# Scale s and offset b moved from the hidden values to the outputs, in a kernel of chunked attention and a squared-ReLU layer

## The chip, the cores and the metric

The kernel runs on one core of a Trainium2 chip. A core has a matrix engine (TensorE, in the profile PE, with its weight loads as PEld), a vector engine (VectorE, DVE), an engine for pointwise functions (ScalarE, ACT), a general engine (GpSimd, POOL) and an engine that here only issues DMAs (SyncE, SP). Each engine works through its own instructions in the order in which they were written and waits on semaphores for the others. The metric is the device time of one execution in microseconds (us); lower is better. The profile speaks of the span, which runs from the first to the last instruction of one profiled execution.

## The reference, cut to what matters

```
# attention: 4 batches, 8 heads, 768 positions of 64; chunks of 32 queries,
# each sees 16 positions to the left, its own 32, 8 to the right, and 8 memory slots
scores = scale * q_c @ k_full.T ;  a = softmax(scores) ;  attn = a @ v_full
x = attn as (3072 tokens, 512)
# the layer
h = x @ w_in                    # 512 -> 2048
r = maximum(h, 0)
g = s * (r * r) + b             # s and b are single numbers
out = g @ w_out                 # 2048 -> 512
```

Since s and b are single numbers, g @ w_out equals s * ((r * r) @ w_out) + b * (column sums of w_out). Nothing in the reference changes; this identity is what the change rests on.

## The kernel before, in words

**Tiling.** The 3072 tokens are eight chunks of 384 (`TOK`), and the 2048 hidden values are sixteen blocks of 128 (`NF`). A step is a pair (chunk, block). `STEPS` runs chunk 0 with blocks 0 to 7, then chunk 1 with all sixteen, then chunk 0 with blocks 8 to 15, then chunks 2 to 7 with all sixteen: 128 steps. In a step, `hidden(u)` makes the 128 x 384 hidden block on PE (L510, 12 matmuls of 384 columns), and ACT takes it through relu (L517), square (L518), s and b (L519, called affine) and a rounding to the short float type into gH (L520). DVE then makes the rest gL, which is the block minus gH (L521). `result(u)` multiplies gH and gL by the block's 128 rows of w_out and adds into three accumulator banks, one for each 128 tokens (L532, 9 matmuls of 512 columns). Every matrix stands as a high and a low part of the short float type, so that three products give nearly full precision: low times high, high times low, high times high.

**Order on PE.** `result` comes one `hidden` late: in steady work the order is hidden(k), result(k-1), hidden(k+1), result(k). So between the end of hidden(k) and the start of result(k) PE has a result and a hidden of other steps to do, while ACT and DVE make gH(k) and gL(k).

**Weights.** Both matrices arrive as 64-bit floats. For each of the 32 blocks of 128 rows (sixteen of each matrix, `weight()`), a DMA brings the words into one of four `words` buffers (the first ten use other space, `early`), and five instructions join the two halves into a 32-bit float and split it: ACT scales (L487), DVE shifts, joins and sets the sign (L488, L490, L492), ACT rounds into the high part (L496), and DVE subtracts to get the low part (L497). These blocks are made while chunks 0 and 1 are already computed.

**Attention.** For each chunk and pair of heads: scores on PE (L383), mask and row maximum on DVE (L440, two instructions for each of eight tiles), exp with row sums on ACT (L444), a small add on POOL (L447), a reciprocal on DVE (L449), the division on POOL (L450, called norm, 96 x 512), a transposition (on PE for chunks 0 and 1, on DVE for the later ones, L470), the value product on PE (L415), and the split into xH and xL (L419 on ACT, L420 on DVE).

**What sets the order.** The program hands all operations to a planner (`Plan`), each with its engine, a hold time from a table (`HOLD`), a due time, the values it reads and writes, and sometimes a flag `lock`. `lay()` walks through time and on each free engine starts the ready operation with the smallest due time; the instructions are then written in the order of their planned starts. With `lock`, an operation of DVE and one of POOL are not started while the other's locked one is running in the plan. The flag is on POOL's L447 and L450 and on DVE's four weight operations. It only orders: no semaphore keeps the two apart on the chip. Tiles come from rings with a fixed number of buffers and are given out in the order in which the values were created. The eight banks of PSUM are one ring `ps` whose function `room` limits each kind: accumulators three, hidden blocks (h) two, scores (s) and attention values (v) together three.

**End of a chunk.** When a chunk's last step is done, DVE copies the three accumulators out (L548) and SP writes them. Chunk 0 is broken in two: after its block 7 ACT stores the partial sums (L543), and after block 15 DVE adds them to the second half (L550).

Of the kernel before, what the change touches and what calls it, by code (L numbers as in the profile page):

```python
# [47 lines left out]
LEAD = 3.5  # L48
BANKS = 8
ORDER = sorted((f + half, half, f) for f in range(NF) for half in range(2))  # L50
LATE_W = [x[1:] for x in ORDER[-NEARLY:]]

# [8 lines left out]
            low=475, affine_v=475, rec=120, max=212, flip=316, xlow=470, wlow=345, wjoin=610, wsign=612, out=600,  # L61
            small=240, norm=1010, wrest=1290, issue=440)
LATE = dict(PE=230, ACT=180, DVE=180, POOL=150, SP=0)
# [182 lines left out]
def body(ctx: ExitStack, tc: tile.TileContext, qkv, w1, w2, out):  # L246
# [7 lines left out]
    def ring(name, n, shape, dtype):  # L254
        return Ring([const.tile(shape, dtype, name=f"{name}{i}") for i in range(n)])
# [27 lines left out]
    gs = Ring([(const.tile([P, TOK], F32R, name=f"gH{i}"), const.tile([P, TOK], F32R, name=f"gL{i}")) for i in range(3)])  # L283
    outs = ring("partial", 3, [P, DM], F32)

    spare = [BANKS - 1]

# [20 lines left out]

    c_id, c_aT, c_mask, c_s, c_b = (fixed() for _ in range(5))
    op("ACT", "copy", -100, lambda: nc.scalar.activation(s_sb, ones[:, :1], AF.Exp), (), (c_s[0],))  # L310
# [188 lines left out]


    g_vals, h_vals, a_vals, partial = {}, {}, {}, {}

    def hidden(u):
        ch, f = STEPS[u]
        h = Val(ps, "h")
        x, w = x_vals[ch], c_w[0, f]

        def products(c):
            for n, (wi, xi) in enumerate(((0, NC_T + c), (1, c), (0, c))):
                nc.tensor.matmul(h.tile[:, :TOK], weight_tile(0, f)[:, wi, c * P:(c + 1) * P], x.tile[xi], start=(c == 0 and n == 0),  # L510
                                 stop=(c == NC_T - 1 and n == 2))

        for c in range(NC_T):
            op("PE", "hidden", u, lambda c=c: products(c), (x["H", c], x["L", c], w["H"], w["L"]), (h[0],))
        g = g_vals[u] = Val(gs)
        hp = lambda: h.tile[:, :TOK]
        op("ACT", "relu", u, lambda: nc.scalar.activation(hp(), hp(), AF.Relu), (), (h[0],))  # L517
        op("ACT", "square", u, lambda: nc.scalar.activation(hp(), hp(), AF.Square), (), (h[0],))  # L518
        op("ACT", "affine", u, lambda: nc.scalar.activation(hp(), hp(), AF.Identity, scale=s_sb, bias=b_sb), (c_s[0], c_b[0]), (h[0],))  # L519
        op("ACT", "high", u, lambda: nc.scalar.activation(g.tile[0], hp(), AF.Copy), (h[0],), (g["H"],))  # L520
        op("DVE", "low", u, lambda: nc.vector.tensor_tensor(g.tile[1], hp(), g.tile[0].bitcast(F32), ALU.subtract),  # L521
           (h[0], g["H"]), (g["L"],))

    def result(u):
# [9 lines left out]
        for t in range(NT):  # L534
# [6 lines left out]
            if f < NF - 1:  # L541
                o = partial[t] = Val(outs)
                op("ACT", "store", u, lambda acc=acc, o=o: nc.scalar.activation(o.tile, acc.tile, AF.Copy), (acc[0],), (o[0],))  # L543
                continue
            o = partial[t] if not ch else Val(wvs if ch == 1 else outs)
            ot = lambda o=o: o.tile
            if ch:
                op("DVE", "out", u, lambda acc=acc, ot=ot: nc.vector.tensor_copy(ot(), acc.tile), (acc[0],), (o[0],))  # L548
            else:
                op("DVE", "out", u, lambda acc=acc, ot=ot: nc.vector.tensor_tensor(ot(), acc.tile, ot(), ALU.add), (acc[0],), (o[0],))  # L550
            row = ch * TOK + t * P
# [6 lines left out]
    for i, (due, half, f) in enumerate(ORDER):  # L558
        weight(i, half, f, due - 1.5)
    for u, (ch, f) in enumerate(STEPS):  # L560
        if ch not in made:
# [52 lines left out]
```

## Time and profile before

| what | value |
|---|---|
| three timed runs | 641.42, 642.25, 642.20 us; median 642.2 |
| span of the profiled execution | 639.8 us |
| what lies around a span | 1.6 us to the fastest run, 2.4 us to the median; the profiled execution's own time is not listed |
| ACT busy | 422.4 us (66%), of which the affine (L519) 82.6 us |
| DVE busy | 354.8 us (55%) |
| POOL busy | 86.9 us (14%) |
| granted TensorE clock | 1.000 |

A row of the groups view names line, engine, operation, output<-inputs, the shape and the count, and then busy us, mean ns of one, idle time of the engine just before them and what ended it. A row of the timeline gives the start in us, the duration in us, engine, line, operation, and in square brackets the idle time before it with its releaser. Matmuls are pipelined: the starts of successive matmuls say more than their durations, and the same holds for DVE, where an instruction starts about 0.1 us before the one ahead of it is over.

### The profile page before, as it was taken

The numbers are of one execution on the slowest core, as the hardware profiler recorded it, in microseconds if no ns is written. First come the engines' busy times: TensorE is split into PE (matmuls) and PEld (weight loads), VectorE is DVE, ScalarE is ACT, GpSimd is POOL, SyncE is SP. The second block draws the span as 40 slices with busy tenths as digits, with TensorE's granted clock in tenths as the row PEclk, the third lists the DMA queues.
The fourth block names the chain that finished last, engine by engine and source line by source line (L and its number), as shares of the span: only waits on it lengthen the run. The fifth ranks groups of instructions, "written<-read, shape, count | busy, mean of one in ns | idle before, by whom it ended". The sixth has DMA issues, their size and how long they took to land.

```text
span 639.8 us, 10842 instructions
## 1 busy us (share of the span) xinstructions
PE 625.7 (98%) x3822; PEld 544.2 (85%) x3826; DVE 354.8 (55%) x1283; ACT 422.4 (66%) x1137; POOL 86.9 (14%) x140
## 2 busy tenths in 40 slices
PE   9998988999999999999999999999999999999997
PEld 5686877888888898888888988889888888989995
DVE  5999999726667355563447554473555725421112
ACT  6999898756766566666566666664666665645543
POOL 4522100101211011110011111110111100100000
PEclk9999999999999999999999999999999999999999
DMA  8933664012112011121103011120111200010001
GB/s 336 404 112 114 212 207 152 2 46 83 58 46 96 5 41 47 47 95 47 45 2 105 37 46 46 46 96 1 45 47 47 96 17 1 1 50 1 1 0 50
DMA packets 17334, 46.83 MB, mean 73 GB/s; under 512 B 1920, under 2 KB 1920, under 8 KB 17280
## 3 DMA queue, kind: packets, MB, share of 16 engines
q1 hardware_dynamic: 17280, 46.15, 20.8%
q8 instruction: 30, 0.49, 0.3%
q14 instruction: 24, 0.20, 0.1%
HBM read 39.85 MB, written 6.29 MB: 72 GB/s over the span
## 4 chain that ended last, share of the span: by engine, by line
PE 80%; DVE 10%; ACT 6%; DMA 4%; issue 1%; SPq 0%; POOL 0%; DVEq 0%
PE ps L532 37%; PE ps L510 36%; PE ps L383 4%; PE ps L415 3%; DVE wv L490 2%; DVE w L497 2%; DVE wv L492 2%; DMA early<-w 2%; ACT t L444 1%; DMA v<-qkv 1%; DVE gL L521 1%; DVE words L488 1%; ACT wv L487 1%; DMA early<-qkv 1%; ACT ps L519 1%; ACT w L496 1%
## 5 line engine op out<-in xcount | busy, mean ns | idle before, releaser
L510 PE MATMUL ps<-xH,w 128*128 128x384 f32 x1024 | 261.8, 337 | 1.3 <-DVE w L497 1.3
L532 PE MATMUL ps<-w,gH 128*128 128x512 f32 x768 | 240.0, 393 | 0.6 <-DVE w L497 0.5
L510 PEld LDWEIGHTS ps<-xH,w 128*128 128x128 f32 x1024 | 186.0, 188 | 7.6 <-DVE w L497 2.4
L521 DVE TENSOR_TENSOR gL<-ps,gH 128x384 fp32r<-128x384 f32 x128 | 70.6, 552 | 208.8 <-ACT gH L520 207.6
L517 ACT ACTIVATE ps<-ps 128x384 f32<-128x384 f32 x128 | 60.9, 475 | 173.1 <-PE ps L510 173.1
L510 PE MATMUL ps<-xL,w 128*128 128x384 f32 x512 | 174.4, 341 | 0.0
L532 PEld LDWEIGHTS ps<-w,gH 128*128 128x128 f32 x768 | 144.0, 188 | 29.4 <-DVE w L497 1.3
L532 PE MATMUL ps<-w,gL 128*128 128x512 f32 x384 | 154.9, 403 | 6.6 <-DVE gL L521 6.6
L470 DVE STREAM_TRANSPOSE aT<-t 32x128 f32<-32x128 f32 x384 | 116.2, 303 | 51.1 <-POOL t L450 46.4
L444 ACT ACTIVATE t<-t,nmax 96x128 f32<-96x128 f32 x256 | 99.3, 390 | 17.2 <-DVE nmax L440 16.9
L510 PEld LDWEIGHTS ps<-xL,w 128*128 128x128 f32 x512 | 96.1, 188 | 6.6 <-ACT w L496 0.4
L532 PEld LDWEIGHTS ps<-w,gL 128*128 128x128 f32 x384 | 72.0, 188 | 24.5 <-DVE gL L521 9.6
L519 ACT ACTIVATE ps<-ps,b_sb,s_sb 128x384 f32<-128x384 f32 x128 | 82.6, 645 | 4.2
L450 POOL TENSOR_TENSOR t<-t,rden 96x512 f32<-96x512 f32 x64 | 68.5, 1070 | 85.8 <-DVE rden L449 85.8
L447 POOL TENSOR_SCALAR rden<-den 96x4 f32<-96x4 f32 x64 | 16.0, 251 | 375.5 <-ACT t L444 372.8
L520 ACT ACTIVATE gH<-ps 128x384 fp32r<-128x384 f32 x128 | 62.9, 491 | 3.9
L518 ACT ACTIVATE ps<-ps 128x384 f32<-128x384 f32 x128 | 60.8, 475 | 4.0
L440 DVE CUSTOM_DVE_ANT_0 t<-ps,mask 96x128 f32<-96x128 f32 x256 | 56.8, 281 | 4.2 <-PE ps L383 3.8
L444 ACT ACTIVATION_READ_ACCUMULATOR t<-t,nmax 96x1 f32 x256 | 48.1, 188 | 0.0
L383 PE MATMUL ps<-raw 64*96 64x128 f32 x448 | 31.8, 279 | 0.0
L383 PEld LDWEIGHTS ps<-raw 64*96 64x96 f32 x448 | 25.3, 159 | 4.1 <-issue 0.8
L415 PEld LDWEIGHTS ps<-aT,v 128*64 128x64 f32 x448 | 19.6, 136 | 7.9 <-issue 6.6
(45 smaller groups left out, 289.3 us busy)
## 6 DMA issues: line engine op xcount, KB each, us to landing
raw<-qkv SPq DMA_DIRECT2D x28, 448.0 KB, 3.3
words<-w SPq DMA_DIRECT2D x22, 512.0 KB, 3.9
v<-qkv SPq DMA_DIRECT2D x28, 256.0 KB, 3.6
out<-partial SPq DMA_DIRECT2D x21, 256.0 KB, 2.1
early<-w SPq DMA_DIRECT2D x10, 512.0 KB, 9.9
early<-qkv SPq DMA_DIRECT2D x3, 448.0 KB, 5.8
early<-qkv SPq DMA_DIRECT2D x4, 256.0 KB, 6.4
out<-wv SPq DMA_DIRECT2D x3, 256.0 KB, 3.8
```

The source lines that it names most:

```text
L383: nc.tensor.matmul(scv(n)[:, j, :], raw.tile[rows, j * QB:(j + 1) * QB], raw.tile[rows, TOK + j * P:TOK + (j + 1) * P], start=True, stop=True)
L440: op("DVE", "max", a + 0.1, lambda j=j: nc.vector.tensor_tensor_reduce(t.tile[:, j, :], scv()[:, j, :], mask[:, kind(j)], -SCALE, 3.0e38, ...
L444: op("ACT", "exp", a + 0.2, lambda j=j: nc.scalar.activation(t.tile[:, j, :], t.tile[:, j, :], AF.Exp, bias=nmax()[:, j:j + 1], scale=-1.0 ...
L450: op("POOL", "norm", a + 0.25, lambda: nc.gpsimd.tensor_tensor(t.tile, t.tile, rden().unsqueeze(2).to_broadcast([QB, GB, P]), ALU.mult), [ ...
L470: nc.vector.transpose(aT.tile[gg, :, cs], t.tile[cs, :, gg])
L510: nc.tensor.matmul(h.tile[:, :TOK], weight_tile(0, f)[:, wi, c * P:(c + 1) * P], x.tile[xi], start=(c == 0 and n == 0), stop=(c == NC_T - ...
L517: op("ACT", "relu", u, lambda: nc.scalar.activation(hp(), hp(), AF.Relu), (), (h[0],))
L518: op("ACT", "square", u, lambda: nc.scalar.activation(hp(), hp(), AF.Square), (), (h[0],))
L519: op("ACT", "affine", u, lambda: nc.scalar.activation(hp(), hp(), AF.Identity, scale=s_sb, bias=b_sb), (c_s[0], c_b[0]), (h[0],))
L520: op("ACT", "high", u, lambda: nc.scalar.activation(g.tile[0], hp(), AF.Copy), (h[0],), (g["H"],))
L521: op("DVE", "low", u, lambda: nc.vector.tensor_tensor(g.tile[1], hp(), g.tile[0].bitcast(F32), ALU.subtract), (h[0], g["H"]), (g["L"],))
L532: nc.tensor.matmul(acc.tile, g.tile[gi][:, t * P:(t + 1) * P], weight_tile(1, f)[:, wi, :], start=(first and n == 0), stop=(last and n == 2))
```

## The change

- L519, the affine on ACT, is gone from every step. The block that goes to `result` is now just the square.
- s is multiplied in where an accumulator leaves PSUM: in the copy of chunk 0's partial sums on ACT, and in the output instruction on DVE, which becomes a scalar_tensor_tensor (accumulator times s plus a tile).
- The tile `bc` holds b times the column sums of w_out, the same in all 128 partitions. It is made once, by the new function `sums()`: fifteen additions on POOL, of 128 x 1024 each (high and low part side by side), add the sixteen blocks of w_out into a tile `total` from the ring `words`; two matmuls with a matrix of ones ("columns") add over the partitions into one PSUM bank; and one activation on ACT multiplies by b into `bc`.
- That bank has a kind of its own, `"sum"`, so that it stands in no queue with the value banks; in `room` it falls under the last line, the one for hidden blocks.
- The outputs of chunks 1 to 7 add `bc` in the DVE instruction. Chunk 0's second half adds its partial sums there, so `bc` is added by POOL in a further instruction of 128 x 512 for each of three tiles, and SP writes the tile after that.
- The planner's table gets `sum=2150` and `columns=1706`, and all these operations have the due time `DUE_SUM = 24.0`, step 24 being the first after chunk 1. The fifteen additions and the three later ones carry `lock`.

```
+DUE_SUM = 24.0
...
+    def sums():
+        total, all_ = Val(words), Val(ps, "sum")
+        flat = lambda f: weight_tile(1, f).bitcast(F32).rearrange("p a n -> p (a n)")
+        part = lambda f: (c_w[1, f]["H"], c_w[1, f]["L"])
+        op("POOL", "sum", DUE_SUM, lambda: nc.gpsimd.tensor_tensor(total.tile, flat(0), flat(1), ALU.add), part(0) + part(1), (total[0],), lock=True)
+        for f in range(2, NF):
+            op("POOL", "sum", DUE_SUM, lambda f=f: nc.gpsimd.tensor_tensor(total.tile, total.tile, flat(f), ALU.add), part(f), (total[0],), lock=True)
+        def products():
+            for a in range(2):
+                nc.tensor.matmul(all_.tile, ones_f, total.tile[:, a * DM:(a + 1) * DM], start=a == 0, stop=a == 1)
+        op("PE", "columns", DUE_SUM, products, (total[0],), (all_[0],))
+        op("ACT", "store", DUE_SUM, lambda: nc.scalar.activation(bc, all_.tile, AF.Identity, scale=b_sb), (all_[0], c_b[0]), (c_bc[0],))
...
-        op("ACT", "affine", u, lambda: nc.scalar.activation(hp(), hp(), AF.Identity, scale=s_sb, bias=b_sb), (c_s[0], c_b[0]), (h[0],))
...
-                op("ACT", "store", u, lambda acc=acc, o=o: nc.scalar.activation(o.tile, acc.tile, AF.Copy), (acc[0],), (o[0],))
+                op("ACT", "store", u, lambda acc=acc, o=o: nc.scalar.activation(o.tile, acc.tile, AF.Identity, scale=s_sb),
+                   (acc[0], c_s[0]), (o[0],))
...
-                op("DVE", "out", u, lambda acc=acc, ot=ot: nc.vector.tensor_copy(ot(), acc.tile), (acc[0],), (o[0],))
+                op("DVE", "out", u, lambda acc=acc, ot=ot: nc.vector.scalar_tensor_tensor(ot(), acc.tile, s_sb, bc, ALU.mult, ALU.add),
+                   (acc[0], c_s[0], c_bc[0]), (o[0],))
...
-                op("DVE", "out", u, lambda acc=acc, ot=ot: nc.vector.tensor_tensor(ot(), acc.tile, ot(), ALU.add), (acc[0],), (o[0],))
+                op("DVE", "out", u, lambda acc=acc, ot=ot: nc.vector.scalar_tensor_tensor(ot(), acc.tile, s_sb, ot(), ALU.mult, ALU.add),
+                   (acc[0], c_s[0]), (o[0],))
+                op("POOL", "norm", u + 1, lambda ot=ot: nc.gpsimd.tensor_tensor(ot(), ot(), bc, ALU.add), (c_bc[0],), (o[0],), lock=True)
...
+    sums()
```

Because the planner sees other hold times, it also writes the rest in another order. SP's order is the same as before. On PE a few transpositions, score and value products of the first 70 us change places with neighbouring matmuls, and the order of hidden and result stays, with columns as the one addition. On DVE and ACT many neighbours change places until the weights are done; DVE's first 294 rows hold the same instructions as before, in another order. In the changed kernel the lines are shifted: L440 is L443, L449 is L452, L450 is L453, L488, L490 and L492 are L491, L493 and L495, L497 is L500, L510 is L530, L521 is L540, L532 is L551.

The first place is DVE, near the end of the weights. Before, from the last use of the buffer words_102 on (the low and high words of block 13 of w_out):

```order
L492 SCALAR_TENSOR_TENSOR wv_98<-words_102,wv_98 128x512
L497 TENSOR_TENSOR w_14_1235<-wv_97,w_14_1235 128x512
L521 TENSOR_TENSOR gL_131<-ps_141,gH_130 128x384
L497 TENSOR_TENSOR w_13_1248<-wv_98,w_13_1248 128x512
L488 TENSOR_SCALAR words_103<-words_103 128x512
L490 SCALAR_TENSOR_TENSOR wv_99<-wv_99,words_103 128x512
L492 SCALAR_TENSOR_TENSOR wv_99<-words_103,wv_99 128x512
L488 TENSOR_SCALAR words_100<-words_100 128x512
L490 SCALAR_TENSOR_TENSOR wv_97<-wv_97,words_100 128x512
L492 SCALAR_TENSOR_TENSOR wv_97<-words_100,wv_97 128x512
L497 TENSOR_TENSOR w_15_1275<-wv_99,w_15_1275 128x512
L521 TENSOR_TENSOR gL_133<-ps_143,gH_132 128x384
```

After that gL_133 come the low part of block 14, the three joins of the last block, gL_129, and the maxima of chunk 2's first pair of heads. In the changed kernel the same place reads as follows; ahead of these rows stand the last use of words_102, gL_131 and six of the seven maxima (L443).

```order
L443 ISA t_107,nmax_119<-ps_140,mask 96x128
L443 ISA nmax_119 96x1
L540 TENSOR_TENSOR gL_133<-ps_142,gH_132 128x384
L500 TENSOR_TENSOR w_13_1237<-wv_98,w_13_1237 128x512
L491 TENSOR_SCALAR words_103<-words_103 128x512
L493 SCALAR_TENSOR_TENSOR wv_99<-wv_99,words_103 128x512
L495 SCALAR_TENSOR_TENSOR wv_99<-words_103,wv_99 128x512
L491 TENSOR_SCALAR words_100<-words_100 128x512
L493 SCALAR_TENSOR_TENSOR wv_97<-wv_97,words_100 128x512
L500 TENSOR_TENSOR w_15_1298<-wv_99,w_15_1298 128x512
L495 SCALAR_TENSOR_TENSOR wv_97<-words_100,wv_97 128x512
```

Seven maxima and gL_133 have moved ahead of twelve weight instructions; behind those twelve (the eight shown and four of the last block and block 14) stand gL_129 and gL_131 of the next two steps, then the two reciprocals rden_118 and rden_121.

The second place is POOL, behind its last division for chunk 1. Before, the next rows were the small adds (L447) and divisions (L450) of chunk 2; in the changed kernel (L450 and L453) the additions of `sums()`, L509 and L511, stand among them:

```order
L509 TENSOR_TENSOR words_102<-w_0_548,w_1_597 128x1024
L511 TENSOR_TENSOR words_102<-words_102,w_2_674 128x1024
L450 TENSOR_SCALAR rden_118<-den_117 96x4
L450 TENSOR_SCALAR rden_121<-den_120 96x4
L511 TENSOR_TENSOR words_102<-words_102,w_3_712 128x1024
L453 TENSOR_TENSOR t_106<-t_106,rden_118 96x512
L453 TENSOR_TENSOR t_107<-t_107,rden_121 96x512
L511 TENSOR_TENSOR words_102<-words_102,w_4_804 128x1024
```

`total` is the buffer words_102, so the first addition waits for the last use of that buffer by DVE and ACT. After the last row shown come nine more additions (blocks 5 to 13), the small add of chunk 2's second pair of heads, the addition of block 14, that pair's first division, a small add, the addition of block 15, and the second division.

The third place is PE, at the end of chunk 1. Before, `result` of block 14 (L532) was followed at once by `hidden` of chunk 0's block 8 (L510); now columns, L515, stands between:

```order
L551 MATMUL ps_141<-w_14_1316,gL_131 128x512
L551 MATMUL ps_141<-w_14_1316,gH_130 128x512 x2
L515 MATMUL ps_145<-words_102,const-float32-1.0 128x512 x2
L530 MATMUL ps_140<-xL_0_85,w_8_966 128x384
L530 MATMUL ps_140<-xH_0_81,w_8_966 128x384 x2
```

Columns reads `total`, so PE comes to `hidden` only when POOL's fifteenth addition is done.

More of the change, by code (lines that the diff above doesn't have):

```diff
@@ L61 @@
             low=475, affine_v=475, rec=120, max=212, flip=316, xlow=470, wlow=345, wjoin=610, wsign=612, out=600,
-            small=240, norm=1010, wrest=1290, issue=440)
+            small=240, sum=2150, columns=1706, norm=1010, wrest=1290, issue=440)
 LATE = dict(PE=230, ACT=180, DVE=180, POOL=150, SP=0)
@@ L284, in body @@
     outs = ring("partial", 3, [P, DM], F32)
+    bc = const.tile([P, DM], F32, name="bc")
+    ones_f = nc.const_aps.tensor(1.0, [P, P], F32)
     spare = [BANKS - 1]
@@ L306, in warm @@
         nc.tensor.matmul(idle, ones[:, :P], ones, start=True, stop=True)
-    c_id, c_aT, c_mask, c_s, c_b = (fixed() for _ in range(5))
+    c_id, c_aT, c_mask, c_s, c_b, c_bc = (fixed() for _ in range(6))
     op("ACT", "copy", -100, lambda: nc.scalar.activation(s_sb, ones[:, :1], AF.Exp), (), (c_s[0],))
```

## The prediction

> **What bounds the kernel now.** The page comes first, then the busy times by stretch.
>
> ```profile
> span 639.8 us, 10842 instructions
> PE 625.7 (98%) x3822; PEld 544.2 (85%) x3826; DVE 354.8 (55%) x1283; ACT 422.4 (66%) x1137; POOL 86.9 (14%) x140
> ```
>
> ```profile
> 25.00:65.00 40.00, 37.33 (x258) 30.14 (x257) 37.59 (x113) 39.51 (x112) 11.45 (x13) 1.00 0.48 169
> 65.00:107.00 42.00, 38.48 (x211) 32.29 (x209) 39.76 (x74) 36.85 (x73) 1.83 (x2) 1.00 0.61 207
> 107.00:113.00 6.00, 4.46 (x22) 3.78 (x22) 5.79 (x12) 5.00 (x11) 0.00 (x0) 1.00 0.06 22
> 113.00:240.00 127.00, 126.20 (x771) 111.81 (x773) 71.34 (x280) 81.14 (x225) 17.60 (x28) 1.00 0.14 47
> 240.00:640.00 400.00, 395.38 (x2357) 351.62 (x2353) 183.45 (x700) 239.90 (x634) 42.73 (x68) 1.00 0.12 41
> ```
>
> The columns after the length are PE, PEld, DVE, ACT and POOL, each with its count. PE looks busy everywhere, but the counts tell more: from 65 to 107 it does 211 matmuls in 42 us, 5.0 per us; from 113 to 240 it does 771 in 127 us, 6.1 per us, and 5.9 to the end. So there are stages. From 25 to 65 ACT is full (39.5 of 40) and DVE nearly; from 65 to 113 DVE is (39.8 of 42, 5.8 of 6), making weights; from 113 on PE is the bound, and ACT and DVE have 40% to spare. The affine's 82.6 us on ACT lie mostly where ACT waits for PE anyway. **Only three things can move the end:** what comes before 113 us, what is added to PE's own queue, and the tail.
>
> **Term 1, the early stages.** What DVE loses there is what a faster ACT can give back; the waits of DVE between 24 and 107 us, and four kinds of ACT's instructions between 24 and 69 us, the affines (L519) among them:
>
> ```profile
> DVE w L497 <- ACT w L496: 1.7, 3, 1.2
> DVE gL L521 <- ACT gH L520: 0.9, 2, 0.7
> DVE rden L449 <- POOL rden L447: 0.3, 1, 0.3
> ```
>
> ```profile
> L444 ACT ACTIVATE t<-t,nmax 96x128 f32<-96x128 f32 x28 | 10.9, 394 | 0.1
> L519 ACT ACTIVATE ps<-ps,b_sb,s_sb 128x384 f32<-128x384 f32 x7 | 4.5, 644 | 0.2
> L520 ACT ACTIVATE gH<-ps 128x384 fp32r<-128x384 f32 x7 | 3.4, 486 | 0.1
> L517 ACT ACTIVATE ps<-ps 128x384 f32<-128x384 f32 x7 | 3.3, 478 | 0.0
> ```
>
> DVE waited 2.9 us in all, every time behind ACT (the POOL wait too: that add waits for exp). Its instructions up to the place where POOL's sums begin are the same ones, and it is nearly full, so it can gain no more than these 2.9 us, though seven affines leave ACT 4.5 us freer. The new order may wait elsewhere, so the ends are 0 and -2.9; I take three quarters, **-2.2**.
>
> **Term 2, the sums against the last weights.** DVE's last weights, and PE's results that hang on them:
>
> ```profile
> 107.04 0.55 DVE L521 TENSOR_TENSOR gL<-ps,gH 128x384 fp32r<-128x384 f32 x1
> 107.51 0.68 DVE L497 TENSOR_TENSOR w<-wv,w 128x512 fp32r<-128x512 f32 x1
> 112.36 0.55 DVE L521 TENSOR_TENSOR gL<-ps,gH 128x384 fp32r<-128x384 f32 x1
> 115.22 0.55 DVE L521 TENSOR_TENSOR gL<-ps,gH 128x384 fp32r<-128x384 f32 x1
> 115.69 0.28 DVE L440 CUSTOM_DVE_ANT_0 t<-ps,mask 96x128 f32<-96x128 f32 x1
> 115.90 0.28 DVE L440 CUSTOM_DVE_ANT_0 t<-ps,mask 96x128 f32<-96x128 f32 x1
> ```
>
> ```profile
> 107.64 0.50 PE L532 MATMUL ps<-w,gL 128*128 128x512 f32 x1 [0.88 <-DVE gL L521]
> 112.97 0.50 PE L532 MATMUL ps<-w,gL 128*128 128x512 f32 x1 [0.89 <-DVE gL L521]
> 117.25 0.39 PE L532 MATMUL ps<-w,gL 128*128 128x512 f32 x1
> ```
>
> Before, twelve weight instructions ran from 107.51 to 115.22 with one gL of 0.47 inside (pitch 115.69 - 115.22), so they take 7.24. In the new order, from 107.04: gL 0.47, seven maxima of 0.21 (pitch 115.90 - 115.69) 1.47, gL 0.47, twelve weight instructions 7.24, gL 0.55: 117.24. PE starts that step's result at 117.3 against 117.25 before. The move alone is free, but it uses up the 1.5 us that this gL had in hand: **from here on each us that DVE loses in this stretch goes to the end.** And POOL is now busy beside it. Rows in which the two meet:
>
> ```profile
> 36.73 1.04 POOL L450 TENSOR_TENSOR t<-t,rden 96x512 f32<-96x512 f32 x1 [1.15 <-DVE rden L449]
> 39.52 1.52 POOL L450 TENSOR_TENSOR t<-t,rden 96x512 f32<-96x512 f32 x1 [0.29 <-DVE rden L449]
> 34.87 0.71 POOL L447 TENSOR_SCALAR rden<-den 96x4 f32<-96x4 f32 x1 [5.56 <-ACT t L444]
> 39.02 0.22 POOL L447 TENSOR_SCALAR rden<-den 96x4 f32<-96x4 f32 x1 [1.25 <-ACT t L444]
> ```
>
> ```profile
> 34.82 0.69 DVE L490 SCALAR_TENSOR_TENSOR wv<-wv,early 128x512 int32<-128x512 int32 x1
> 35.54 0.69 DVE L492 SCALAR_TENSOR_TENSOR wv<-early,wv 128x512 int32<-128x512 int32 x1
> 36.83 0.56 DVE L521 TENSOR_TENSOR gL<-ps,gH 128x384 fp32r<-128x384 f32 x1 [0.18 <-ACT gH L520]
> 37.35 0.97 DVE L497 TENSOR_TENSOR w<-wv,w 128x512 fp32r<-128x512 f32 x1
> 39.45 0.69 DVE L490 SCALAR_TENSOR_TENSOR wv<-wv,early 128x512 int32<-128x512 int32 x1
> ```
>
> The division takes 1.04 alone, and 1.52 when a DVE weight instruction (39.45 to 40.14) is ahead of it; DVE's L497 takes 0.97 instead of 0.68 when a division (to 37.77) is ahead of it: it ends 0.55 after that. So one blocks the other. The small add, 0.22 alone, took 0.71 while L490 ran and ended at 35.58: it got in between two DVE weight instructions that follow each other.
>
> Now the sums. One is 128 x 1024, twice the division's length: 2.08 by its row. The first begins when DVE is through with words_102, just ahead of the gL of 107.04, and runs beside gL and maxima, which read PSUM and meet no one (gL at 36.83 beside the same division kept its 0.56). It ends near 109.2; the second runs to 111.3. DVE is through with its second gL at 109.6 (109.45 by the count, plus 0.15 for ACT, which rounds block 13 near 107.1 to 107.6 and then needs 1.5 for relu, square and gH, half a us each), and then wants its first weight instruction: it waits **1.7**. POOL's next two rows are small adds that wait for ACT's seven exps behind that gH (109.1 + 7 x 0.39, over near 112); then the third sum comes, in the midst of the weight instructions. If it gets in between two of them as the small add did, DVE waits a further **2.1**. After it POOL stands at a division whose reciprocal is behind DVE's weights, so no fourth sum can come. Ends: 0 (no blocking) and 4.2 (two whole sums); I take 1.7 + 2.1 = **+3.8**, as both kinds of meeting are in the rows.
>
> [...]
>
> **Term 3, columns on PE.** No row shows this product: 32-bit floats, two matmuls of 512 columns. Nearest are the scores, also plain 32-bit:
>
> ```profile
> 139.10 1.12 PE L383 MATMUL ps<-raw 64*96 64x128 f32 x16
> 140.14 0.50 PE L532 MATMUL ps<-w,gL 128*128 128x512 f32 x1
> 150.74 0.34 PE L510 MATMUL ps<-xL,w 128*128 128x384 f32 x1
> ```
>
> Eight score matmuls of 128 columns take 1.04 (140.14 - 139.10), in 16 records, two for each. That is 1024 columns, as many as columns has. If the scores, which use 64 of the 128 rows each, run two side by side, the full product costs double: ends 1.0 and 2.1. I take **+1.8**, since successive scores lie in different halves of the rows. It stands at 150.74, in the stage in which PE is full, so nothing hides it.
>
> [...]
>
> **Term 4, the tail.**
>
> ```profile
> 134.15 2.10 PE ps L532 x9
> 631.97 0.65 ACT L519 ACTIVATE ps<-ps,b_sb,s_sb 128x384 f32<-128x384 f32 x1
> 632.65 0.49 ACT L520 ACTIVATE gH<-ps 128x384 fp32r<-128x384 f32 x1
> 633.78 0.50 PE L532 MATMUL ps<-w,gL 128*128 128x512 f32 x1 [0.76 <-DVE gL L521]
> ```
>
> The last result waits 0.76 for gL, and gH starts 0.68 after the affine does. Without it PE starts 0.68 sooner: **-0.7**, sure within 0.1.
>
> **Costed at nothing.** POOL's fifteen sums: the first three end by 115.2, the next ten need 21 us from the two divisions on (122 to 144), and the last two stand around the second pair's division, which follows PE's scores. With both blocks they are over about 1.4 us before PE comes to columns; if POOL is later, PE waits for each us. The output instruction:
>
> ```profile
> L548 DVE COPY partial<-ps 128x512 f32<-128x512 f32 x18 | 11.7, 686 | 3.3 <-PE ps L532 3.2
> L550 DVE TENSOR_TENSOR partial<-ps,partial 128x512 f32<-128x512 f32 x3 | 1.9, 685 | 0.0
> ```
>
> A copy takes 686 ns and an add of PSUM and SBUF 685, so the new form adds nothing at the tail (bound: 0.1). POOL's three additions for chunk 0 (1.04 each) make SP write these tiles up to 3 us later and hold up the loads behind them on SP, which are wanted a group of steps later, over 10 us on. The activation that makes `bc` and the scaled copies on ACT lie where ACT has room.
>
> **The sum:** -2.2 + 3.8 + 1.8 - 0.7 = **+2.7**. It is made on the span, 639.8 to 642.5; what lies around a span (2.4 to the median) stays, so 642.2 becomes **644.9**.
>
> **Rivals.** (a) *The third sum does not get in*: DVE's instructions start 0.1 us before the last is over, so POOL might find no gap. Against it stands the small add of 34.87. Then term 2 is 1.7 and the time 642.8, within 0.2%. (b) *No blocking that counts, and the early gain whole*: the sums begin later, or DVE's gL waits hide them; -2.9 + 0 + 1.8 - 0.7 = -1.8, 640.4, faster. It decides the sign: with the whole early gain the kernel gets faster where DVE is blocked for less than 1.8 us, and measurably so below 0.5. Against it stand the 0.97 and 1.52. (c) *The early gain fails*: DVE in its new order waits for weights that ACT has not rounded; 0 + 3.8 + 1.8 - 0.7 = +4.9, 647.1. (d) *The change does not do what it says*: L519 is gone from ACT's order, so this is not likely; nothing in PE's bound stage depends on it.
>
> **How the numbers follow.** About 0.2%, 1.3 us, is what a measurement of this kernel can tell from no change. Chances: forecast 0.45, (a) 0.25, (b) 0.17, (c) 0.13. The forecast is slower by more than 1.3 unless terms 1 to 3 are all at their friendly ends (0.36 slower, 0.09 same); (a) is mostly the same (0.05 slower, 0.18 same, 0.02 faster); (b) 0.12 faster, 0.05 same; (c) slower. That gives faster 0.14, same 0.32, slower 0.54. The bounds alone make -2.6 (-2.9 + 0 + 1.0 - 0.7) to +5.6 (0 + 4.2 + 2.1 - 0.7): 639.6 to 647.8. The range leaves a tenth at each end: 640.2 to 647.4.
>
> **What would show it.** Right: the second and third L511 beside a DVE weight instruction of over 2 us in place of 0.69, and a wait of PE of some 4 to 5 us for gL just behind; columns taking 1.8 on PE with no wait for POOL ahead of it; DVE's waits for ACT ahead of that under 1 us; the last result waiting 0.1. Wrong: weight instructions at 0.69 beside the sums, or PE waiting at columns for POOL, or a longer stretch before the sums begin, with DVE waiting for ACT or PE.

## The result, and the profile after

The changed kernel takes **648.8 us** (median of 4 runs, 648.4 to 649.5) against 642.2 before: 6.6 us, a ratio of 1.0103 (95% interval 1.0088 to 1.0117). Forecast were 644.9, with a range to 647.4. The sign was right, the size was not. The execution shown here took 648.89 us.

First two lines of the page, its row of granted clocks (40 slices of 16.2 us), and the longest of PE's waits (sum in us, times, longest).

```profile
span 647.0 us, 10742 instructions
PE 630.9 (98%) x3830; PEld 548.1 (85%) x3830; DVE 361.8 (56%) x1283; ACT 343.0 (53%) x1010; POOL 127.6 (20%) x158
PEclk9999989899999999999999999999999999999999
```

```profile
PE ps L551 <- DVE gL L540: 9.4, 5, 5.4
```

The affine's 80 us are gone from ACT, POOL has 41 us more, and PE is still the bound. Two things are new: one wait of 5.4 us, and two slices in which PE's clock was not full. Before, no wait for gL was over 0.9 us:

```profile
PE ps L532 <- DVE gL L521: 6.6, 9, 0.9
```

The place, on POOL, DVE and PE in the changed kernel:

```profile
108.52 2.40 POOL L509 TENSOR_TENSOR words<-w,w 128x1024 f32<-128x1024 f32 x1 [39.45 <-ACT wv L490]
110.99 2.92 POOL L511 TENSOR_TENSOR words<-words,w 128x1024 f32<-128x1024 f32 x1
115.08 2.82 POOL L511 TENSOR_TENSOR words<-words,w 128x1024 f32<-128x1024 f32 x1
125.89 24.74 POOL L511 TENSOR_TENSOR words<-words,w 128x1024 f32<-128x1024 f32 x10
```

```profile
110.97 0.68 DVE L500 TENSOR_TENSOR w<-wv,w 128x512 fp32r<-128x512 f32 x1
111.56 2.63 DVE L491 TENSOR_SCALAR words<-words 128x512 int32<-128x512 int32 x1
114.95 0.69 DVE L495 SCALAR_TENSOR_TENSOR wv<-words,wv 128x512 int32<-128x512 int32 x1
115.56 2.62 DVE L491 TENSOR_SCALAR words<-words 128x512 int32<-128x512 int32 x1
120.03 0.42 DVE L491 TENSOR_SCALAR words<-words 128x512 int32<-128x512 int32 x1
122.29 1.01 DVE L540 TENSOR_TENSOR gL<-ps,gH 128x384 fp32r<-128x384 f32 x2
```

```profile
122.90 0.79 PE L551 MATMUL ps<-w,gL 128*128 128x512 f32 x1 [5.37 <-DVE gL L540]
123.49 1.05 PE L551 MATMUL ps<-w,gH 128*128 128x512 f32 x2
157.94 1.88 PE L515 MATMUL ps<-words,const-float32-1.0 128*128 128x512 f32 x4
```

The second and the third sum each stand beside a DVE instruction of 2.6 us that takes 0.42 when alone and ends 0.3 us after the sum: 2.2 us lost twice, 4.4. Each sum starts while a DVE weight instruction is running (L500, L495), is 0.4 to 0.5 us longer than the 2.40 of the first one, and gets in ahead of the next weight instruction. PE's result starts at 122.90, 5.65 later than before's at 117.25. What follows wasn't foreseen: two matmuls on gH take 1.05 instead of 0.63. Windows of 2 us, the column before the last two being the granted clock:

```profile
122.00:124.00 2.00, 1.10 (x3) 0.91 (x4) 2.00 (x6) 0.81 (x2) 0.53 (x1) 0.69 0.00 0
124.00:126.00 2.00, 2.00 (x6) 1.56 (x5) 1.03 (x5) 0.00 (x0) 2.00 (x3) 0.50 0.00 0
126.00:128.00 2.00, 2.00 (x12) 1.86 (x11) 1.12 (x4) 0.00 (x0) 2.00 (x1) 0.96 0.00 0
```

From 124 to 126 PE does the matmuls of 6 records at clock 0.50, in the next window those of 12 at 0.96. The three rows together are worth 3.4 us at half clock ((1 - 0.69) x 4 + 2.0 + (1 - 0.96) x 4). In before's trace the clock never falls until the last matmul is done: its one fall is at 639.53 us.

**Where the time went.** ACT's first instruction of a step (relu) stands once in each of the 128 steps, so before and after can be laid beside each other step by step:

| relu of step | before, us | after, us | later by | what lies between |
|---|---|---|---|---|
| 0 | 30.03 | 30.94 | 0.91 | the start |
| 14 | 107.72 | 108.95 | 1.23 | early stages: +0.3 |
| 17 | 121.63 | 128.85 | 7.22 | two shut-out weights 4.4, PE's slow clock 1.55 |
| 23 | 148.84 | 156.04 | 7.20 | nothing |
| 24 | 153.05 | 161.96 | 8.91 | columns: +1.7 |
| 28 | 174.94 | 182.82 | 7.88 | a wait of before that is gone: -1.0 |
| 127 | 630.96 | 638.84 | 7.88 | nothing: 400 us at one pitch |

The tail gives back 0.6: the last result waits 0.1 us and starts 0.67 sooner after its relu, and the three outputs behind it take 0.06 longer. That leaves 7.3 of the 7.88; the spans, 639.8 and 647.0, differ by 7.2. The 1.0 is a wait that before had in the stage that PE bounds:

```profile
164.22 0.50 PE L532 MATMUL ps<-w,gL 128*128 128x512 f32 x1 [0.80 <-DVE gL L521]
```

It stood behind exps, the affine and 2.5 us of transposes; in the changed kernel's order no such wait is left. The affine alone didn't make it: in the run below that keeps the old order without the affine, a wait of 0.64 stays there. The 0.91 at the start is not the change's. Sixteen score matmuls, the same in both, took 1.12 us before and 2.03 after. The full clock is first on record at 4.65 us before and at 6.71 after, so the fast sixteen stand behind that entry and the slow sixteen ahead of it; which clock was granted ahead of it is not on record:

```profile
4.70 1.12 PE L383 MATMUL ps<-early 64*96 64x128 f32 x16
```

```profile
4.70 2.03 PE L386 MATMUL ps<-early 64*96 64x128 f32 x16
```

In the twelve profiles below the first relu stands anywhere from 29.5 to 30.9; shifts below are taken from each run's own start.

### The profile page after: what moved, and what is told of

Same layout as the page of the kernel before. It is cut to its first block, busy times and chain, and to the rows that moved or that the text cites. A ratio compares the mean times of both kernels' runs of the same rounds, so it can differ in the third digit from the quotient of the medians.

```text
span 647.0 us, 10742 instructions
## 1 busy us (share of the span) xinstructions
PE 630.9 (98%) x3830; PEld 548.1 (85%) x3830; DVE 361.8 (56%) x1283; ACT 343.0 (53%) x1010; POOL 127.6 (20%) x158
## 4 chain that ended last, share of the span: by engine, by line
PE 85%; DVE 10%; ACT 4%; issue 0%; DVEq 0%
PE ps L551 38%; PE ps L530 37%; PE ps L386 5%; PE ps L418 3%; DVE wv L493 2%; DVE w L500 2%; DVE wv L495 2%; PE ps L309 2%; DVE words L491 1%; DVE gL L540 1%; ACT t L447 1%; DVE t L443 1%; ACT w L499 1%; ACT ps L538 1%; ACT gH L539 1%; ACT wv L490 1%
## 5 line engine op out<-in xcount | busy, mean ns | idle before, releaser
L530 PE MATMUL ps<-xH,w 128*128 128x384 f32 x1024 | 262.4, 337 | 1.9 <-DVE w L500 1.8
L551 PE MATMUL ps<-w,gH 128*128 128x512 f32 x768 | 241.5, 396 | 0.0
L530 PEld LDWEIGHTS ps<-xH,w 128*128 128x128 f32 x1024 | 186.5, 188 | 8.5 <-DVE w L500 3.1
L540 DVE TENSOR_TENSOR gL<-ps,gH 128x384 fp32r<-128x384 f32 x128 | 70.5, 552 | 209.5 <-ACT gH L539 208.3
L530 PE MATMUL ps<-xL,w 128*128 128x384 f32 x512 | 175.2, 342 | 0.0
L551 PEld LDWEIGHTS ps<-w,gH 128*128 128x128 f32 x768 | 145.2, 189 | 28.6 <-DVE w L500 0.3
L551 PE MATMUL ps<-w,gL 128*128 128x512 f32 x384 | 155.6, 405 | 9.5 <-DVE gL L540 9.4
L447 ACT ACTIVATE t<-t,nmax 96x128 f32<-96x128 f32 x256 | 99.4, 390 | 18.2 <-DVE nmax L443 18.2
L530 PEld LDWEIGHTS ps<-xL,w 128*128 128x128 f32 x512 | 96.3, 188 | 6.9 <-ACT w L499 0.5
L551 PEld LDWEIGHTS ps<-w,gL 128*128 128x128 f32 x384 | 72.5, 189 | 26.5 <-DVE gL L540 11.5
L453 POOL TENSOR_TENSOR t<-t,rden 96x512 f32<-96x512 f32 x64 | 68.5, 1070 | 83.0 <-DVE rden L452 82.9
L450 POOL TENSOR_SCALAR rden<-den 96x4 f32<-96x4 f32 x64 | 16.1, 252 | 301.1 <-ACT t L447 298.2
L443 DVE CUSTOM_DVE_ANT_0 t<-ps,mask 96x128 f32<-96x128 f32 x256 | 57.0, 281 | 5.1 <-PE ps L386 4.7
L447 ACT ACTIVATION_READ_ACCUMULATOR t<-t,nmax 96x1 f32 x256 | 48.2, 188 | 0.0
L511 POOL TENSOR_TENSOR words<-words,w 128x1024 f32<-128x1024 f32 x14 | 34.6, 2470 | 1.0
```

Of the source, the lines that this page charges most:

```text
L443: op("DVE", "max", a + 0.1, lambda j=j: nc.vector.tensor_tensor_reduce(t.tile[:, j, :], scv()[:, j, :], mask[:, kind(j)], -SCALE, 3.0e38, ...
L447: op("ACT", "exp", a + 0.2, lambda j=j: nc.scalar.activation(t.tile[:, j, :], t.tile[:, j, :], AF.Exp, bias=nmax()[:, j:j + 1], scale=-1.0 ...
L453: op("POOL", "norm", a + 0.25, lambda: nc.gpsimd.tensor_tensor(t.tile, t.tile, rden().unsqueeze(2).to_broadcast([QB, GB, P]), ALU.mult), [ ...
L551: nc.tensor.matmul(acc.tile, g.tile[gi][:, t * P:(t + 1) * P], weight_tile(1, f)[:, wi, :], start=(first and n == 0), stop=(last and n == 2))
```

## The experiments

Three theories had to be told apart: the sums did it (shutting DVE out, then the clock, then columns); the planner's new order did it; or the early gain is simply not to be had. Times are medians, beside those of the kernel before on the same chip.

| run | us | before | ratio, 95% interval |
|---|---|---|---|
| late sums (one meets a weight) | 644.21 | 641.69 | 1.0029 to 1.0054 |
| no sums | 639.78 | 641.69 | 0.9960 to 0.9979 |
| no affine, old order, no sums | 639.84 | 641.69 | 0.9959 to 0.9979 |
| before plus sums | 655.70 | 641.69 | 1.0205 to 1.0233 |
| no sum meets a weight | 644.13 | 642.02 | 1.0021 to 1.0046 |
| pause filled at 117 | 647.37 | 642.02 | 1.0073 to 1.0101 |
| folded | 640.80 | 642.02 | 0.9974 to 0.9992 |
| no sums, no early divisions | 639.48 | 642.02 | 0.9954 to 0.9979 |
| no sums, pause filled at 83 | 640.03 | 642.17 | 0.9955 to 0.9980 |
| no sum meets, filled at 83 | 643.85 | 642.17 | 1.0017 to 1.0039 |
| folded, old order | 641.93 | 642.17 | 0.9991 to 1.0009 |
| neither divisions nor pause | 639.98 | 641.84 | 0.9955 to 0.9978 |

**Later sums.**

```diff
-... flat(0), flat(1), ALU.add), part(0) + part(1), (total[0],), lock=True)
+... flat(0), flat(1), ALU.add), part(0) + part(1) + part(NF - 1), (total[0],), lock=True)
```

> The changed kernel, except that POOL's first sum also waits for the last weight block, and the planner's price of a sum is 2450 instead of 2150 ns, so that columns stand late enough on PE. Theory A (from the two traces: 4.4 us because two sums shut out two of DVE's weight instructions, 1.55 us because PE's granted clock falls to 0.5 after the 5.4 us that PE waits for it): both go, 648.8 - 5.95 = 642.9 us, DVE's weight instructions at 0.42 and 0.69, no PE wait over 2 us near 117. Theory B (the new order of the instructions costs the time, whatever POOL does): 647 to 649. Theory C (blocking yes, but the fall of the clock belongs to the place and not to the wait): 648.8 - 4.4 = 644.4.

644.2: the number of theory C, but not for its reason. The plan put the first sum behind the last weight, yet nothing in its data made it wait, so it still ran early, and the second only after the weights:

```profile
107.08 2.40 POOL L509 TENSOR_TENSOR words<-w,w 128x1024 f32<-128x1024 f32 x1 [39.28 <-ACT wv L490]
119.45 2.39 POOL L511 TENSOR_TENSOR words<-words,w 128x1024 f32<-128x1024 f32 x1 [0.15 <-POOL rden L450]
```

```profile
107.33 2.43 DVE L491 TENSOR_SCALAR words<-words 128x512 int32<-128x512 int32 x1
```

```profile
114.49 0.50 PE L551 MATMUL ps<-w,gL 128*128 128x512 f32 x1 [2.58 <-DVE gL L540]
```

```profile
114.00:116.00 2.00, 1.51 (x7) 1.25 (x8) 1.97 (x4) 1.93 (x4) 0.00 (x0) 1.00 0.04 8
```

One sum, one weight instruction shut out for 2.0 us, a PE wait of 2.58, and here no fall of the clock. So one meeting costs 2.0 to 2.2 and two cost 4.4, as term 2's mechanism wants; columns again moved the steps by 1.7 (relu 24 to 25).

**The affine's going by itself, in the new order and in the old.** First the sums and columns are left out; then the affine is also kept in the plan, with nothing issued for it, and POOL's three additions for chunk 0 go too.

```diff
+        nc.gpsimd.memset(bc, 0.0)
...
-    sums()
```

```diff
+        op("ACT", "affine", u, lambda: None, (c_s[0], c_b[0]), (h[0],))
```

> The changed kernel without the sums, the columns product and its activation; bc is filled with 0, so b times the column sums is left out of the output. It shows what the affine's going is worth by itself. If the 1.26 us that the changed kernel had lost by 107 us belong to the new order: 648.8 - 4.4 - 1.55 - 1.7 = 641.2 us. If the early gain of the prediction comes through without the sums: 642.2 - 2.2 - 0.7 = 639.3.

> As the run without sums (b times the column sums left out of the output, no POOL additions for chunk 0), but the planner still counts the affine at its old place and length and nothing is issued for it: every engine keeps the order of the kernel before, only the affine is gone from ACT. If the early gain was eaten by the new order: 642.2 - 2.2 - 0.7 = 639.3 us or less, since before's own PE wait of 0.8 at 164 should shrink as well. If DVE's early waits were never what set the end (PE is): the tail alone, 642.2 - 0.7 = 641.5, and the changed kernel's order would be innocent.

Both are 1.9 us faster than before, so the affine's going is worth 1.9, and the sums cost 8.5 (6.6 + 1.9). But the 1.9 comes in different places. In the old order the early gain is there: relu stands 0.63 later at step 0 and 0.99 earlier from step 10 to 24, 1.6 won. In the new order it isn't: 0.04 earlier at step 0, 0.02 later at step 17, nothing won; instead the wait at 164 goes, 1.0. Three rows of the run without sums show DVE where it used to wait for ACT:

```profile
37.27 1.35 DVE L501 TENSOR_TENSOR w<-wv,w 128x512 fp32r<-128x512 f32 x1
50.94 1.09 DVE L492 TENSOR_SCALAR early<-early 128x512 int32<-128x512 int32 x1
64.26 1.08 DVE L492 TENSOR_SCALAR words<-words 128x512 int32<-128x512 int32 x1
```

Alone these take 0.69, 0.42 and 0.42; each stands beside one of POOL's divisions, and 2.0 us are lost in them, where before lost 0.3 in one. (The run in the old order lost 1.2 in three such instructions and still gained.) Its chain of work goes on through PE at 83:

```profile
83.11 0.79 PE L552 MATMUL ps<-w,gL 128*128 128x512 f32 x1 [2.45 <-DVE gL L541]
83.70 1.05 PE L552 MATMUL ps<-w,gH 128*128 128x512 f32 x2
```

```profile
84.00:86.00 2.00, 2.00 (x6) 1.52 (x6) 1.86 (x4) 1.75 (x4) 0.00 (x0) 0.50 0.67 199
86.00:88.00 2.00, 2.00 (x11) 1.82 (x10) 1.97 (x5) 1.21 (x3) 0.00 (x0) 0.88 0.79 246
```

A PE wait of 2.45 us that before doesn't have, and a fall of the clock behind it. The changed kernel has both as well, and the three long DVE instructions too:

```profile
84.04 0.50 PE L551 MATMUL ps<-w,gL 128*128 128x512 f32 x1 [2.42 <-DVE gL L540]
```

So two suspects for the lost gain: divisions that shut DVE out, and the clock.

**The sums by themselves**, added to the kernel before, affine and all:

```diff
+    bc = const.tile([P, DM], F32, name="bc")
+    sums()
```

> The kernel before, affine and all, with the fifteen sums, the columns product and its activation added; their result is used by nothing. Theory A: the blocking, the fall of the clock and columns come with the sums, whatever ACT does: 642.2 + 4.4 + 1.55 + 1.7 = 649.9 us (647.5 if only one weight instruction is shut out). If the blocking needs the new order of the changed kernel: 642.2 + 1.8 = 644.0.

655.7, 14.0 over before and 6 more than expected. 5.8 come at the weights (steps 14 to 17). The rest is a way that was costed at nothing: POOL late for the next pair's softmax.

```profile
152.46 0.17 DVE L452 RECIPROCAL rden<-rden 96x4 f32<-96x4 f32 x1 [3.43 <-POOL rden L450]
155.96 2.52 DVE L473 STREAM_TRANSPOSE aT<-t 32x128 f32<-32x128 f32 x8 [3.32 <-POOL t L453]
158.60 0.52 DVE L541 TENSOR_TENSOR gL<-ps,gH 128x384 fp32r<-128x384 f32 x1
```

```profile
159.18 0.80 PE L552 MATMUL ps<-w,gL 128*128 128x512 f32 x1 [4.19 <-DVE gL L541]
```

```profile
160.00:162.00 2.00, 2.00 (x6) 1.52 (x6) 1.92 (x7) 0.00 (x0) 0.00 (x0) 0.50 0.00 0
```

DVE waits 3.4 and 3.3 us for a small add and a division that stand behind sums on POOL; gL stands behind both on DVE; PE waits 4.2 and then runs at clock 0.50. With columns, 7.7 us there. In the changed kernel POOL ended its last sum 0.7 us before PE came to columns: it was that close.

**No sum meets a weight, and the pause filled.** In one kernel the blocks are summed from 15 and 14 on, so that the data hold the first sum back. In the other, 20 products of constants stand on PE ahead of the result that waits 5.4 us.

```diff
-        ... flat(0), flat(1) ... for f in range(2, NF):
+        ... flat(NF - 1), flat(NF - 2) ... for f in range(NF - 2):
```

```diff
+        if u == 15:
+            spot = Val(ps, "fill")
+            op("PE", "fill", u + LAG - 0.2, lambda: [nc.tensor.matmul(spot.tile, ones[:, :P], ones, start=True, stop=True) for _ in range(20)],
+               (g["H"], g["L"], w["H"], w["L"]), (spot[0],))
```

> The changed kernel with the blocks summed in another order, 15 and 14 first, so that POOL's first sum can't begin before DVE's last weight is written (in the run with late sums one sum still met one weight instruction, since only the plan, not the data, made it wait); the planner's price of a sum is 2450 ns. Theory A (each sum that meets a weight instruction costs about 2 us, columns 1.7): against the run with late sums, 2.5 us over before, another 2.0 go, and the time is within 1 us of before, 641.5 to 642.7. Rival (POOL, busy later, holds up the second pair's divisions and with them DVE's transposes and gL, as in the run with sums only): 644 to 647, with a PE wait over 2 us between 150 and 165.

> The changed kernel with 20 products of constants, 128x512 each, into a free bank, placed on PE just ahead of the result that waits 5.4 us for gL near 117; they wait for nothing, and the planner counts them at 1 ns, so that all other orders stay. Theory (the granted clock falls because PE pauses): the clock stays at 1.00 through the pause, the matmuls behind it run at full pitch, and 1.55 us are won: 648.8 - 1.55 = 647.3. Rival (the matmuls behind the pause are slow for another reason, or the clock falls all the same): no change, 648.5 to 649.

The filled pause came out as the clock theory had it, 647.4. PE's wait is 1.03 instead of 5.37, the clock stays whole, and matmuls behind it are at full pitch:

```profile
116.01 4.55 PE L556 MATMUL ps<-const-bfloat16-1.0 128*128 128x512 bf16 x20
121.59 0.50 PE L552 MATMUL ps<-w,gL 128*128 128x512 f32 x1 [1.03 <-DVE gL L541]
121.92 0.63 PE L552 MATMUL ps<-w,gH 128*128 128x512 f32 x2
155.98 1.98 PE L516 MATMUL ps<-words,const-float32-1.0 128*128 128x512 f32 x4 [0.67 <-POOL words L512]
```

At step 17, measured from each start, it is 1.6 ahead of the changed kernel; columns then waits 0.67 for POOL, which is no earlier, and gives 0.9 of it back. So 20 matmuls that compute nothing win 1.6 us at their place in the trace. In the medians, measured apart, 1.2 is left (648.8 and 647.4), with intervals of the ratios that overlap.

With no meeting, DVE's instructions at 112 to 117 are all 0.42 and 0.69, and PE has no long wait there; yet the run took 644.1, not 642: the rival's time, but without the rival's PE wait of over 2 us between 150 and 165. In the execution that was profiled (644.45), the pause at 83 (2.54 us) is followed by two stretches of half clock instead of one, which makes relu 1.4 late by step 17:

```profile
82.00:84.00 2.00, 1.29 (x3) 1.10 (x4) 1.90 (x5) 1.94 (x5) 0.00 (x0) 0.53 0.27 107
84.00:86.00 2.00, 2.00 (x6) 1.52 (x6) 1.97 (x4) 1.76 (x4) 0.00 (x0) 0.50 0.77 254
86.00:88.00 2.00, 2.00 (x8) 1.81 (x7) 1.93 (x5) 0.85 (x2) 0.00 (x0) 0.50 0.77 254
```

Columns cost 2.6, with a wait of 0.34 for POOL; and the wait that the changed kernel lost at 164 is back (0.67). The longer fall was this execution's: its mean granted clock is 0.994, those of the other four are 0.996 and 0.997, which is one stretch. The median does without it: nothing won early (as in the run without sums), columns +2.6, the tail -0.6, together +2.0, and 2.1 were measured.

**What ate the early gain?** Four kernels: without the early divisions; with 9 products ahead of the result at 83, without and with the sums; and with both covers gone. The filler is the one above, for step 8.

```diff
-        op("POOL", "norm", a + 0.25, lambda: nc.gpsimd.tensor_tensor(
+        op("POOL", "norm", a + 0.25, lambda: None if bare else nc.gpsimd.tensor_tensor(
```

```diff
-        if u == 15:  ... range(20)
+        if u == 8:  ... range(9)
```

> The run without sums, and also without POOL's divisions of the first two chunks (their softmax weights stay unnormalised, and b times the column sums is left out, so the output is another one); the plan still counts them. In the run without sums three of DVE's weight instructions before 107 us take 1.35, 1.09 and 1.08 us in place of 0.69 and 0.42, each beside a division. Theory (these 2.0 us are where the early gain went): DVE's last weight ends about 2 us sooner and the time is 639.8 - 2.0 = 637.8, at least 1.3 under the run without sums. Rival (PE or the loads set that stage): 639.5 to 640.

> The run without sums (b times the column sums left out), with 9 products of constants on PE, 2.1 us, ahead of the result that waits 2.45 us for gL at 83; they wait for nothing and the planner counts them at 1 ns, so that all other orders stay. In the trace of the run without sums the granted clock is 0.50 for 3.41 us from there on, and the chain that ends last goes through PE's matmuls in it (3.88 us for nine in place of 2.10). Theory (this fall of the clock is what ate the early gain in the new order, so 1.8 us): no fall at 83, 639.8 - 1.8 = 638.0 us. Rival (the loss is DVE's, in instructions shut out by divisions and in waits for ACT, and PE only shares it): 639.3 to 640.

> The run in which no sum meets a weight, complete, with the same 9 products of constants ahead of the result at 83. There the granted clock was 0.50 for 6.83 us. Theory: without it the early stage is 1.6 us shorter than in the kernel before, columns and its wait cost 2.6, the tail gives 0.7: before + 0.3, 641.7 to 642.7. Rival (the loss of that run lies elsewhere): 643.5 to 644.5.

> The run without sums and without the divisions of the first two chunks (their weights stay unnormalised, b times the column sums is left out), and with the 9 products of constants ahead of the result at 83. Alone, the missing divisions gave 0.3 us by 121 us against the run without sums, and the filled pause 0.7, in the traces and with the start's own difference taken off; DVE was shut out for 2.0 us by divisions in one, and PE's clock fell in the other. Theory (two covers, one behind the other, each hides the other's gain; the prediction's 2.2 is there once both are gone): 2.2 to 2.7 us by 121 us against the kernel before, and a time of before - 3.5 to - 4.2. Rival (something else, as ACT or the loads, holds the stage behind both): no more than 1.2 by 121 us, a time of before - 2.0 to - 2.9.

All four theories fell. Without divisions DVE's long instructions are gone, but in their place it waits for gH behind ACT, and 0.3 is won by step 17 instead of 2.0:

```profile
40.62 0.56 DVE L541 TENSOR_TENSOR gL<-ps,gH 128x384 fp32r<-128x384 f32 x1 [0.41 <-ACT gH L540]
54.27 0.56 DVE L541 TENSOR_TENSOR gL<-ps,gH 128x384 fp32r<-128x384 f32 x1 [0.31 <-ACT gH L540]
67.52 0.56 DVE L541 TENSOR_TENSOR gL<-ps,gH 128x384 fp32r<-128x384 f32 x1 [0.65 <-ACT gH L540]
```

With the pause filled the clock never falls, and 0.7 is won. With neither, 0.5. The run without meetings gained 1.6 by step 17 when its pause was filled (from 1.4 late to 0.3 early), but its median only 0.4, since only the profiled one of its executions had the longer fall to lose. The last kernel's chain of work shows ACT's exps and a load of words between DVE's pieces:

```profile
36.75 0.77 ACT t L448 x4
38.42 1.14 ACT wv L491 x2
51.53 1.63 ACT t L448 x8
73.76 4.43 DMA words<-w
78.27 0.68 ACT wv L491
```

So in the new order the early stages seem to rest on several engines by turns: take one cover away and the next is there. DVE's idle time in the 82 us from 25 to 107, shifted by each run's start, bears this out: 4.7 us before, 3.0 in the changed kernel and without sums, 4.3 without divisions, 4.1 with neither, 2.5 in the old order. So in the changed kernel 1.7 us of waiting went, and as much came back in instructions shut out by divisions (2.0 against 0.3); without the divisions most of the waiting is there again. What exactly in that order brings it back stays open; that the order does, and not the lack of something to gain, is shown by the run in the old order, with 1.6.

**Another way without the affine.** c = b / s is added in the steps that make gH and gL, and the outputs are multiplied by s: no sums, no columns (s must not be 0).

```diff
+nc.scalar.activation(g.tile[0], hp(), AF.Identity, bias=c_sb)
+nc.vector.scalar_tensor_tensor(g.tile[1], hp(), c_sb, g.tile[0].bitcast(F32), ALU.add, ALU.subtract)
```

> Another way to do without the affine, complete, for s not 0: c = b / s is made once, gH is the rounding of the square plus c (ACT, with a bias), gL the square plus c minus gH (DVE, one instruction with a scalar), and the outputs are multiplied by s; no sums, no columns, bc is gone. From the run without sums (1.9 us under before) and an instruction on ACT and one on DVE that may be up to 0.15 us longer in each step: 639.8 to 640.3 if these take as long as now; near 642, no better than before, if DVE's instruction gets longer by 0.15 us, since DVE has 16 of them before 116 us, where it is the bound.

> The folded form (c = b / s into gH and gL, outputs times s, no sums), with the affine still counted by the planner at its old place, so that every engine keeps the order of the kernel before. From the run in the old order without sums (1.9 us under before) and 0.1 to 0.6 us for the longer gH and gL: before - 1.3 to - 1.8. If the slow drift of the folded run (1.6 us between 200 and 640, without a wait in any row) belongs to the form, the trace shows it again; if it was that execution's, not.

In its own order this is 1.2 us faster than before, and the only complete kernel here that beats both; in the old order it makes no difference, where 1.3 to 1.8 had been expected. gH takes 582 ns instead of 492, gL 612 instead of 552. Both traces drift: from step 28 to 127 they lose 1.6 us against every other kernel, some 0.04 us in each of seven of a chunk's sixteen steps and nothing in the rest, without a wait in any row. It belongs to the form, since two executions show it; its cause is open.

## Why the prediction was wrong

- **Bound and places:** right. From step 28 on nothing differs, and only the early stages, PE's queue and the tail counted.
- **Term 1, -2.2: failed, +0.3 came.** The step was "three quarters of 2.9". DVE's waits behind ACT did shrink, from 2.9 to about 1.1 us, as told to be looked for. But in the new order DVE ran into POOL's divisions (2.0 us in three instructions, 1.7 more than before), which is as much as DVE's idle time had shrunk by, and PE waited 2.4 us at 84, with a slow clock behind it. With both taken away only 0.5 us came, since most of DVE's waiting was back; why it comes back in that order stays open. The upper end, 0, was named and given too little weight: "its instructions are the same ones" says nothing of their order. The gain itself was real, 1.6 us, in an order that the change didn't keep.
- **Term 2, +3.8: right in mechanism, 4.4 in size.** The forecast had the second sum already running when DVE came, for a wait of 1.7, and only the third getting in between two weight instructions. In the trace both got in between two, and each cost 2.2. A sum takes 2.40 to 2.47 us, not the 2.08 scaled from the division.
- **Not in the sum: PE's clock, +1.55.** The prediction forecast a PE wait of 4 to 5 us and priced it as a delay alone. In the trace the granted clock is 0.50 for 3.41 us from 122.76 on, just before the wait of 5.37 is over, and the filled pause (clock 1.00 from 122 to 128, step 17 earlier by 1.6) shows that the wait is the cause. A shorter one was enough at 84, where the clock fell behind 2.42 us (last section). Two of the changed kernel's four executions have a mean clock of 0.991 and 0.992, less than the 0.995 of the profiled one, and took 648.4 and 649.5 us; what the clock cost in them isn't known.
- **Term 3, +1.8: right**, 1.7, with no wait for POOL, though POOL was done only 0.7 us ahead and not 1.4. **Term 4, -0.7: right within its 0.1**, 0.6: the output instruction, costed at nothing, takes 746 ns in its new form and 686 as a copy.
- **Not in the sum: before's own wait at 164, -1.0.** Its row stood in the trace before, in the stage said to be PE's alone; the count of waits for gL (6.6 us) was not split by place.
- **Rivals:** (c), the early gain fails, was nearest in number, 647.1; with the clock's 1.55, the missing 0.6 of term 2 and the 1.0 given back it makes 648.3. Its reason was another: DVE was to wait for ACT's rounding, and those waits shrank. The terms as measured make +6.35, the difference of the medians is +6.6.

## What to carry to other kernels

PE's waits of 2.4 to 5.4 us shown here cost twice, but for one of 2.58: the time itself, and matmuls at clock 0.50 behind them, worth 1.55 us behind the 5.37. Price the second part whenever a change makes PE wait that long, and look for matmuls to put there: 20 products of constants won 1.6 us back. An engine with idle time isn't free to use where its instructions shut out another engine's: fifteen adds on POOL and one product cost 8.5 us, the 128 affines that they replace 1.9. And when an instruction is taken out of a planner's input, time it once with its place kept and nothing issued: that tells the gain of the work from the price of the new order.

## What was not expected of the hardware

- **The clock fell for 3.41 us at a time, and not behind every long wait.** In the changed kernel's trace it falls at 85.22 and 122.76 us and is whole again 3.41 later each time; counted from the first entry, at 6.71, these are 23 and 34 times 3.413 us, and before's one fall, at 639.53, is 186 times that from 4.65. In the 3.41 us ahead of these three falls PE was idle for 2.24 us (81.80 to 85.22), for 3.41 (119.35 to 122.76) and, behind the last matmul of before, for 3.39. From 115.94 to 119.35 it was idle for 1.82, and the clock stayed at 1.00; in every other such stretch of the two traces, from the first entry to the last result, it was idle for 0.9 or less. A wait by itself doesn't tell: behind that of 2.58 us at 114, in the run with late sums, the clock was 1.00, behind that of 2.45 at 83, in the run without sums, 0.50. Nor does the kernel: of the ten executions without sums, eight have a mean clock of 0.996 or 0.997 and two 1.000, and these two are the fastest (639.0 and 639.3 us).
- **Start.** The same sixteen matmuls took 1.12 us before, 1.74 in the run in the old order and 2.03 in the changed kernel, and the first relu of the last two came 0.63 and 0.91 later than before's. Over the fourteen traces the first relu differs by 1.4 us, 0.2% of this kernel.
- **A DVE instruction with one input is shut out too.** In the rows of the prediction the one that a division held up, L497 at 0.97 us in place of 0.68, has two inputs. L491, with one input and an immediate, took 2.63 and 2.62 beside a sum and 0.42 without one.
